# A fused attention and feed-forward kernel: bias rows stored in two goes, sums issued before copies, the first x split by VectorE

## The chip, the cores and the metric

The kernel runs on one core of a Trainium2 chip. Its engines are TensorE (PE in the profile; PEld is its weight load), VectorE (DVE), ScalarE (ACT), GpSimd (POOL) and SyncE (SP), which here only issues transfers. The metric is the device time of one execution in microseconds; a lower time is better.

## What is computed

Attention with a learned bias of position, 4 batches (B), 8 heads (H), 576 positions (S), head size 64 (D), and behind it a gated feed-forward layer over the 2304 resulting rows of 512 features:

```python
scores = scale * np.matmul(q, k.transpose(0, 1, 3, 2))
x = (psi_rel / psi_i)[..., None]
h = np.maximum(x @ w1 + b1, 0.0)
bias = h @ w2                                  # S x S x heads
scores = scores + bias.transpose(2, 0, 1)[None, :, :, :]
attn = np.exp(scores - np.max(scores, axis=-1, keepdims=True))
attn = attn / (np.sum(attn, axis=-1, keepdims=True) + 1e-09)
out = np.matmul(attn, v)                       # (B, H, S, D), then (B*S, H*D) as x
h = x @ w_in
sp = np.log1p(np.exp(h))
y = (h * np.tanh(sp)) @ w_out
```

All arrays are float32. Where full accuracy is wanted, a factor is split into a high and a low part, and a product is three matmuls (high x high, high x low, low x high).

## The kernel before, in words

The program is written out in order, engine by engine: each engine runs its instructions in the order in which the Python code records them, and waits on semaphores. Nothing reorders them. Transfers are issued in order by SP; each waits for one that was issued eight before it to land, and for the data it reads.

**Bias table** (to about 57 us). 36 tiles of 16 positions are made by `make_h` (ACT and DVE), a matmul, and `evac` (L471), which scales the result into a tile `bt` of 128 rows (16 positions x 8 heads) x 591 floats and stores it to `bias_d[c]`, one DRAM tensor for each of the chunks of 128 query positions (the last has 64). The chunks go in `ORDER` 0, 1, 4, 2, 3. `load_bias(hp, c)` reads the two heads of a head pair back; for head pair 0 (heads 0 and 1) the calls stand at the numbers in `BIAS_AT`. The first three steps of the attention already run in here.

**Attention** (to about 320 us). 16 pairs i (head pair, batch), 5 chunks each, so steps n = 0 to 79 (`NS` = 80). Of a step, `scores` (PE) makes the products, `add_bias` (DVE, L209; "the sums" below) adds the bias and takes the row's least value, `exps` (ACT, L224) the exponentials and their totals, `transposes` two steps later turns them on PE and copies them to SBUF (ACT L265, L267, L270, L271; in step 3 one of the copies on DVE), `pv_duo` (PE) multiplies with v, and its result is copied by DVE (L291) and stored to `x_d`. PSUM holds one step's scores and one result at a time. `reciprocals` (DVE L231 to L234) turns a pair's totals into factors, which go to `r_d`. In between, `split` takes a weight through a conversion of DVE steps (L118, L121, L123, L125). Step 3 is written apart: PE's three earlier transposes and the first products are recorded ahead of its sums.

**x for the feed-forward part.** x is worked on in five blocks of 512 tokens (block 2 has 256). `load_x` reads a block, `load_r` its factors, broadcast over 64 partitions; x times the factors is split into `x_hi` and `x_lo`. For block 0 this happens during the last eleven steps of the attention (`ahead`, L327), in halves: POOL multiplies (L346), DVE casts to the high part (L349), POOL subtracts (L350). For the others it happens in the block before (`split_x`, L536; DVE and ACT), load at f = 6 and parts from f = 8 on, f being the number of the unit's first 128 features of 2048.

**Feed-forward part** (from about 310 us). Units of one f (in block 2 two) run through `hidden` (L554), `gate` (L572) and, three units later, `project` (L588). At the end of a block the four results are copied by DVE and ACT in turn and stored; the very last tile is copied in halves by both engines (L611, L612).

Of the kernel before, what the change touches and what calls it, by code (L numbers as in the profile page):

```python
# [19 lines left out]
P = 128  # L20
# [24 lines left out]
def kernel(ctx: ExitStack, tc, qk, v, wb, w2, w_in, w_out, psia, psi4, rinv, eye, out):  # L45
# [101 lines left out]
    st = lsbuf("st", 6)  # L147
    rawp = rsbuf("raw", 2, side="right")
    biasp = rsbuf("biasp", side="right")
    s_ps = rpsum("s_ps", 2, side="right")  # L150
    qk_raw, v_t, bias_t = {}, {}, {}
    st.tile([P, 32], F32, name="fill", bufs=1)
# [146 lines left out]
    conv = []  # L299
    alloc_weights(order[:EARLY], wpool)  # L300

    x_raw, x_r, x_hi, x_lo = {}, {}, {}, {}
    blocks = [(0, 512), (512, 512), (1024, 256), (1280, 512), (1792, 512)]

    def load_x(blk, p):
# [21 lines left out]
    def ahead(n):  # L327

        i, x = divmod(n, 5)
        if x == 0 and i + 1 < NPAIR:  # L330
            load_raw(i + 1)
        if i % B == B - 1 and i // B + 1 < HP:
            load_bias(i // B + 1, ORDER[x])
        if n == NS - 11:
            load_x(0, x0)
        if n in (NS - 10, NS - 8):
            x_r[0] = x0.tile([P, 2, TB], F32, name="xr", bufs=1)
            h0 = 0 if n == NS - 10 else 2
            load_r(0, x_r[0], h0, h0 + 2)
        if n in (NS - 9, NS - 7):  # L340
            if n == NS - 9:
                x_hi[0] = xa.tile([P, HP, TB], F32R, name="xhi")
                x_lo[0] = xa.tile([P, HP, TB], F32R, name="xlo")
            h0 = 0 if n == NS - 9 else 2
            for d in range(2):
                pool.tensor_tensor(x_raw[0][:, h0 + d], x_raw[0][:, h0 + d], x_r[0][:, d], op=ALU.mult)  # L346
        if n in (NS - 7, NS - 6, NS - 4, NS - 3):
            d = (NS - 7, NS - 6, NS - 4, NS - 3).index(n)
            dve.tensor_copy(x_hi[0][:, d], x_raw[0][:, d])  # L349
            pool.tensor_tensor(x_lo[0][:, d], x_raw[0][:, d], x_hi[0][:, d].bitcast(F32), op=ALU.subtract)  # L350

    def split(n):

# [10 lines left out]
    def step(n):  # L364
        i, x = divmod(n, 5)

        def begin():
            if n < NS:
                scores(n)
                add_bias(n)  # L370
                exps(n, 0)

        def turn():
            if 0 <= n - LAG < NS:
                transposes(n - LAG)

        def end():
            if n < NS:
                ahead(n)
                split(n)  # L380
            if 0 <= n - 1 < NS and (n - 1) % 5 == 4:
                reciprocals((n - 1) // 5)

        def products():
            todo = {4: (i, 0, (0, 1)), 0: (i - 1, 0, (2, 3)), 1: (i - 1, 0, (4,)), 2: (i - 1, 1, (0, 1, 2)),
                    3: (i - 1, 1, (3, 4))}.get(x, (-1, 0, ()))
            j, grp, ks = todo
            if 0 <= j < NPAIR and (j, grp) != (0, 0):
                for k in ks:
                    pv_duo(j, grp, k)  # L390

        if n in (3, 4):
            scores(n)
            if n == 3:
                for k in range(3):
                    transposes(k, True)
                for k in range(5):
                    pv_duo(0, 0, k)
            add_bias(n)
            exps(n, 0)  # L400
            exps(n, 1)
            end()
            return
        begin()
        turn()
        if n < NS:
            exps(n, 1)
        end()
        products()

# [18 lines left out]
    dve.tensor_scalar(bb, psi4_t, wbt[:, 1:2], None, op0=ALU.mult)  # L429
    dve.tensor_scalar(at, at, wbt[:, 0:1], None, op0=ALU.mult)  # L430
    ts = [t for c in ORDER for t in range(8 * c, min(8 * c + 8, S // 16))]
    bps_t, h_t = {}, {}
    NB = len(ts)
    NW = S + 15

# [7 lines left out]
    spent = {"v": 0.0, "a": 0.0}  # L443
    maker = {}
    SOFT_AT = (18, 27, 32)
    BIAS_AT = (12, 20, 24, 36, 37)
    for idx, t in enumerate(ts):
        spent["a"] += 1.0 + (1.9 if idx in SOFT_AT else 0.0)
        spent["v"] += (1.7 if idx in SOFT_AT else 0.0)
# [21 lines left out]
    def evac(idx):  # L471
        t = ts[idx]
        ps = bps_t.pop(t)
        bt = bo.tile([P, NW], F32, name="bt")
        left, right, _ = reach(t)
        if idx > NB - 3:
            dve.tensor_scalar(bt[:, :left], ps[:, left:0:-1], rinv_t[:, t:t + 1], None, op0=ALU.mult)
        else:
            act.mul(bt[:, :left], ps[:, left:0:-1], rinv_t[:, t:t + 1])
        act.mul(bt[:, left:], ps[:, :right], rinv_t[:, t:t + 1])  # L480

        c = t // 8
        a = (16 * t - P * c) * PITCH + PAD - 15
        dst = bias_d[c][:, a:a + 16 * (PITCH + 1)].rearrange("h (i j) -> i h j", j=PITCH + 1)
        sp.dma_start(out=dst[:, :, :NW], in_=bt)

    make_h(0)
    make_h(1)
# [1 line left out]
    for idx in range(NB + 2):  # L490
        if idx < NB:
            t = ts[idx]
            make_h(idx + 2)
            n = reach(t)[2]
            ps = bps.tile([P, 1024], F32, name="bps")
            for a in range(0, n, 512):
                for cg in range(4):
                    pe.matmul(ps[cg * 32:cg * 32 + 32, a:min(a + 512, n)], w2t,
                              h_t[idx, cg][:, a:min(a + 512, n)], start=True, stop=True)
            bps_t[t] = ps  # L500
        if 1 <= idx <= NB:
            evac(idx - 1)
        if idx == 1:
            load_raw(0)
        if idx in BIAS_AT:
            load_bias(0, ORDER[BIAS_AT.index(idx)])
        for lag, do in enumerate((scores, add_bias, exps)):
            if idx - lag in SOFT_AT:
                for u in range(2 if lag == 2 else 1):
                    do(SOFT_AT.index(idx - lag), *((u,) if lag == 2 else ()))  # L510
        if idx == 14:
            load_raw(1)
        if idx == 26:
            load_weights()
    bias_scope.close()

    ptp = lsbuf("ptp", 1)
# [70 lines left out]
    def project(blk, fs):  # L588
# [13 lines left out]
        if fs[-1] == NFC - 1:  # L602
            for t in range(nt):
# [5 lines left out]
                if blk == len(blocks) - 1 and t == nt - 1:  # L609

                    dve.tensor_copy(part[:, :DM // 2], ys[blk][t][:, :DM // 2])  # L611
                    act.copy(part[:, DM // 2:], ys[blk][t][:, DM // 2:])  # L612
                    sp.dma_start(out=rows[:, :DM // 2], in_=part[:, :DM // 2])
                    act.dma_start(out=rows[:, DM // 2:], in_=part[:, DM // 2:])
                    continue
                if t % 2:
                    act.copy(part, ys[blk][t])
# [23 lines left out]
    for k in range(2, len(units) + LAG2):  # L641
        if k < len(units):
            blk, fs = units[k]
            f = fs[0]
            if blk + 1 < len(blocks):
                if f == 6:
                    load_x(blk + 1, xp)
                    x_lo[blk + 1] = (xa if blk % 2 else xp).tile([P, HP, TB], F32R, name="xlo")
                    load_r(blk + 1, x_lo[blk + 1].bitcast(F32), 0, HP)

                if f >= 8:
                    split_x(blk + 1, XPARTS[f - 8:f - 8 + len(fs)])
            if k > 2:
                hidden(blk, fs)
        if k >= LAG2:
            project(*units[k - LAG2])
        if 2 <= k - 1 < len(units):
            gate(*units[k - 1], 2)
# [55 lines left out]
```

## Time and profile before

| | us |
|---|---|
| three runs, median | 723.97 |
| the three runs | 723.97, 726.0, 722.36 |
| the profiled execution, its own time | 719.21 |
| its span, first to last instruction | 717.4 |
| busy: PE | 689.8 |
| busy: DVE, ACT, POOL | 513.1, 480.6, 19.5 |

The span is what the views divide up; 1.8 us of the execution lie around it. Matmuls are pipelined and their ends modelled, so PE's busy time counts a matmul that crawls at a lowered clock as busy too; the granted clock (PEclk, 1.00 is full speed) stands beside it. "Idle before" in a row is the time in which that engine stood still just before the instruction, with what ended it.

### The profile page before, as it was taken

How to read it: one execution, taken by the hardware profiler on the slowest of the kernel's cores; microseconds unless marked ns; L12 is line 12 of the kernel's file. 1: busy time of each engine (PE TensorE's matmuls, PEld its weight loads, DVE VectorE, ACT ScalarE, POOL GpSimd, SP SyncE). 2: the span in 40 equal slices, each digit the busy share in tenths (PEclk: the TensorE clock that was granted, in tenths of full speed). 3: DMA queues.
4: the chain of work that ended last, by engine and by line, in shares of the span. 5: the costliest groups of instructions: out<-in, count | busy, mean ns of one | idle time of the engine just before them, and what ended most of it. 6: DMA issues, size and time to landing. Idle time of an engine off the chain costs nothing.

```text
span 717.4 us, 12816 instructions
## 1 busy us (share of the span) xinstructions
PE 689.8 (96%) x4768; PEld 506.6 (71%) x4768; DVE 513.1 (72%) x1082; ACT 480.6 (67%) x1051; POOL 19.5 (3%) x20
## 2 busy tenths in 40 slices
PE   6778999999999999899999999999999999999997
PEld 2225666666666666568888888889978888888886
DVE  7996887788888787758779665665476567565564
ACT  6886998898899989776666454544454554454443
POOL 0000100000000000501000000000000000000000
PEclk9999999999999999999999999999999999999999
DMA  5996458447646846104000030000604100010001
GB/s 157 323 322 198 178 193 259 157 140 248 206 158 219 262 166 221 47 18 127 1 0 1 1 117 1 0 1 6 172 1 124 24 0 1 1 58 1 1 1 58
DMA packets 43919, 74.79 MB, mean 104 GB/s; under 512 B 13905, under 2 KB 22609, under 8 KB 43857
## 3 DMA queue, kind: packets, MB, share of 16 engines
q1 hardware_dynamic: 43280, 73.75, 31.8%
q8 instruction: 37, 0.61, 0.3%
q10 hardware_dynamic: 576, 0.22, 0.1%
q14 instruction: 26, 0.20, 0.1%
HBM read 53.55 MB, written 20.40 MB: 103 GB/s over the span
## 4 chain that ended last, share of the span: by engine, by line
PE 68%; ACT 12%; DVE 6%; DMA 4%; issue 3%; SPq 1%; POOL 0%; DVEq 0%; ACTq 0%
PE y L600 25%; PE h L562 25%; PE s L193 6%; PE o L284 6%; ACT pt L224 5%; ACT main L265 3%; PE tp L257 3%; DVE pt L209 2%; PE tp L260 1%; PE o L288 1%; DMA r_d<-rt 1%; DMA xlo<-r_d 1%; DMA xraw<-x_d 1%; DMA bias_d<-bt 1%; ACT main L270 1%
## 5 line engine op out<-in xcount | busy, mean ns | idle before, releaser
L209 DVE CUSTOM_DVE_ANT_0 pt<-s,bias 128x576 f32<-128x576 f32 (+1 forms) x160 | 115.8, 754 | 45.2 <-PE s L193 44.0
L224 ACT ACTIVATE pt<-pt,m 128x576 f32<-128x576 f32 x144 | 111.2, 773 | 24.5 <-DVE m L209 19.8
L600 PE MATMUL y<-who,glo 128*128 128x512 f32 x288 | 112.2, 389 | 0.0
L600 PE MATMUL y<-who,ghi 128*128 128x512 f32 x288 | 112.2, 389 | 0.0
L600 PE MATMUL y<-wlo,ghi 128*128 128x512 f32 x288 | 112.1, 389 | 0.0
L193 PE MATMUL s<-rawqk 64*128 64x288 f32 x640 | 109.6, 432 | 2.0 <-DVE m L209 2.0
L584 ACT CAST ghi<-e 128x512 fp32r<-128x512 f32 x72 | 44.7, 621 | 92.6 <-DVE e L580 92.6
L193 PEld LDWEIGHTS s<-rawqk 64*128 64x128 f32 x640 | 64.0, 186 | 44.5 <-DVE m L209 16.5
L567 ACT ACTIVATE e<-h 128x512 f32<-128x512 f32 x72 | 42.9, 596 | 64.0 <-PE h L562 63.7
L585 DVE TENSOR_TENSOR glo<-e,ghi 128x512 fp32r<-128x512 f32 x72 | 49.8, 691 | 44.9 <-ACT ghi L584 44.9
L568 DVE TENSOR_SCALAR e<-e 128x512 f32<-128x512 f32 x72 | 30.6, 425 | 71.6 <-ACT e L567 71.6
L562 PE MATMUL h<-xlo,whi 128*128 128x512 f32 (+1 forms) x320 | 79.3, 368 | 1.0 <-DVE xlo L546 0.9
L562 PE MATMUL h<-xhi,whi 128*128 128x512 f32 (+1 forms) x320 | 79.0, 369 | 0.0
L284 PE MATMUL o<-main,vt 128*64 128x320 f32 (+1 forms) x512 | 75.9, 418 | 3.1 <-DVE x L291 3.1
L562 PE MATMUL h<-xhi,wli 128*128 128x512 f32 (+1 forms) x320 | 78.7, 368 | 0.0
L257 PEld LDWEIGHTS tp<-ident,pt 64*128 64x128 f32 x1184 | 55.9, 139 | 18.0 <-ACT main L265 8.3
L265 ACT COPY main<-tp 128x512 f32<-128x512 f32 x126 | 66.7, 578 | 2.0 <-DMA bias_d<-bt 1.0
L562 PEld LDWEIGHTS h<-xhi,whi 128*128 128x128 f32 x320 | 57.1, 188 | 11.7 <-issue 0.5
L562 PEld LDWEIGHTS h<-xlo,whi 128*128 128x128 f32 x320 | 56.9, 189 | 11.6 <-DVE xlo L546 1.7
L257 PE MATMUL tp<-ident,pt 64*128 64x64 f32 x1184 | 62.0, 227 | 2.6 <-ACT main L265 1.2
L562 PEld LDWEIGHTS h<-xhi,wli 128*128 128x128 f32 x320 | 56.9, 189 | 10.0
L600 PEld LDWEIGHTS y<-who,glo 128*128 128x128 f32 x288 | 54.1, 188 | 11.8 <-DVE glo L585 0.4
(58 smaller groups left out, 890.6 us busy)
## 6 DMA issues: line engine op xcount, KB each, us to landing
rawqk<-in_qk_dram SPq DMA_DIRECT2D x16, 672.0 KB
bias_d<-bt SPq DMA_DIRECT2D x36, 295.5 KB
w<-in_w_in_dram SPq DMA_DIRECT2D x16, 512.0 KB
w<-in_w_out_dram SPq DMA_DIRECT2D x16, 512.0 KB
vt<-in_v_dram SPq DMA_DIRECT2D x16, 320.0 KB
bias<-bias_d SPq DMA_DIRECT2D x16, 288.0 KB
out_dram<-w SPq DMA_DIRECT2D x17, 256.0 KB
bias<-bias_d SPq DMA_DIRECT2D x16, 256.0 KB
```

The source lines that it names most:

```text
L193: pe.matmul(s[:, j, :SH], q[rows], raw[rows, k0 + j * SH:k0 + (j + 1) * SH], start=True, stop=True)
L209: dve.tensor_tensor_reduce(out=halves(pt[rows, sl]), in0=s[rows, :, :SH], in1=halves(bt[rows, sl]), scale=-0.125, scalar=BIG, op0=ALU.add, ...
L224: act.activation(ps, ps, AF.Exp, bias=m[:, u:u + 1], scale=-1.0, accum_out=sums[i][:, k:k + 1])
L257: pe.transpose(tp[:, k * 64:k * 64 + 64], pt[rows, c0:c0 + P], ident[rows, rows])
L265: copy(main[:, :, :, q0:q0 + 64], tp.rearrange("p (h k q) -> p h k q", h=2, k=4))
L284: pe.matmul(o[h * 64:h * 64 + 64, :w], vt[:, h, k, :], main[:, h, k, :], start=(k == 0), stop=False, **kw)
L562: pe.matmul(h[:, u * n:(u + 1) * n], w["i", g4, d][:, r * P:(r + 1) * P], x[:, d, :n], start=(k == 0), stop=(k == 11))
L567: act.activation(e, h, AF.Exp)
L568: dve.tensor_scalar(e, e, E20, None, op0=ALU.min)
L584: act.copy(ghi, e)
L585: dve.tensor_tensor(glo, e, ghi.bitcast(F32), op=ALU.subtract)
L600: pe.matmul(ys[blk][t], g[:, c0:c0 + P], w, start=(f == 0 and k == 0), stop=(f == NFC - 1 and k == 2))
```

## The change

1. **Bias stores.** The last six tiles (numbers 30 to 35, all of chunk 3) lie in a pool of their own, `latep`, which outlives the table. Heads 0 and 1 of each are stored first, by two transfers of 16 rows. All eight heads are stored once more after the loop, behind the load of chunk 3.
2. **`BIAS_AT`.** The load of chunk 2 stands two tiles earlier (34 for 36).
3. **Steps 3 and 4.** The sums of step 3 stand behind the first of three transposes; exponentials and transposes alternate; the first pair's products move to step 4, behind its sums.
4. **`end()`.** Reciprocals are recorded ahead of the step's loads and weight steps.
5. **First x.** One load of all factors, into `x_lo`; at steps 75 to 78 DVE multiplies x by them straight into `x_hi`, POOL multiplies x in place and subtracts.
6. **Last pair.** Its third product of group 0 moves one step up.
7. **Last copy.** ACT's half goes to a tile of its own.
8. **Block 3.** In block 2 the next block's load stands at f = 2 and its parts from f = 6.

```diff
-    BIAS_AT = (12, 20, 24, 36, 37)
+    BIAS_AT = (12, 20, 24, 34, 37)
...
+        late = idx >= NB - 6
+        bt = (latep if late else bo).tile([P, NW], F32, name="late" if late else "bt")
...
-        sp.dma_start(out=dst[:, :, :NW], in_=bt)
+        if late:
+            rows = bt.rearrange("(i h) j -> i h j", h=H)
+            for h in range(2):
+                sp.dma_start(out=dst[:, h, :NW], in_=rows[:, h])
+            again.append((dst[:, :, :NW], bt))
+        else:
+            sp.dma_start(out=dst[:, :, :NW], in_=bt)
...
+    for rows, bt in again:
+        sp.dma_start(out=rows, in_=bt)
     bias_scope.close()
...
             if n == 3:
-                for k in range(3):
-                    transposes(k, True)
+                transposes(0, True)
+            add_bias(n)
+            exps(n, 0)
+            if n == 3:
+                transposes(1, True)
+            exps(n, 1)
+            if n == 3:
+                transposes(2)
+            else:
                 for k in range(5):
                     pv_duo(0, 0, k)
-            add_bias(n)
-            exps(n, 0)
-            exps(n, 1)
             end()
...
+            if 0 <= n - 1 < NS and (n - 1) % 5 == 4:
+                reciprocals((n - 1) // 5)
             if n < NS:
                 ahead(n)
                 split(n)
-            if 0 <= n - 1 < NS and (n - 1) % 5 == 4:
-                reciprocals((n - 1) // 5)
...
-        if n in (NS - 10, NS - 8):
-            x_r[0] = x0.tile([P, 2, TB], F32, name="xr", bufs=1)
-            h0 = 0 if n == NS - 10 else 2
-            load_r(0, x_r[0], h0, h0 + 2)
-        if n in (NS - 9, NS - 7):
...
-            for d in range(2):
-                pool.tensor_tensor(x_raw[0][:, h0 + d], x_raw[0][:, h0 + d], x_r[0][:, d], op=ALU.mult)
-        if n in (NS - 7, NS - 6, NS - 4, NS - 3):
-            d = (NS - 7, NS - 6, NS - 4, NS - 3).index(n)
-            dve.tensor_copy(x_hi[0][:, d], x_raw[0][:, d])
-            pool.tensor_tensor(x_lo[0][:, d], x_raw[0][:, d], x_hi[0][:, d].bitcast(F32), op=ALU.subtract)
+        if n == NS - 10:
+            x_hi[0] = xa.tile([P, HP, TB], F32R, name="xhi")
+            x_lo[0] = xa.tile([P, HP, TB], F32R, name="xlo")
+            load_r(0, x_lo[0].bitcast(F32), 0, HP)
+        if NS - 5 <= n < NS - 1:
+            d = n - (NS - 5)
+            x, hi, lo = (y[0][:, d] for y in (x_raw, x_hi, x_lo))
+            dve.tensor_tensor(hi, x, lo.bitcast(F32), op=ALU.mult)
+            pool.tensor_tensor(x, x, lo.bitcast(F32), op=ALU.mult)
+            pool.tensor_tensor(lo, x, hi.bitcast(F32), op=ALU.subtract)
...
-                if f == 6:
+                early = 2 * (len(fs) - 1)
+                if f == 6 - 2 * early:
                     load_x(blk + 1, xp)
...
-                if f >= 8:
-                    split_x(blk + 1, XPARTS[f - 8:f - 8 + len(fs)])
+                if f >= 8 - early:
+                    split_x(blk + 1, XPARTS[f - 8 + early:f - 8 + early + len(fs)])
```

How the order moves at three places (rows of the built programs; the first column is the line in that version's code, which lies one line lower from the attention on and up to ten lower at the end after the change).

SP at the end of the table, before: `bias_d_81` is chunk 3's tensor, `bias_852` and `bias_856` the loaded chunks 2 and 3.

```order
L485 DMA bias_d_81<-bt 16x8x591 x8
L168 DMA bias_852<-bias_d_80 128x576
L169 DMA bias_852<-bias_d_80 128x512
L170 DMA bias_852<-bias_d_80 128x64
L168 DMA bias_856<-bias_d_81 128x576
L169 DMA bias_856<-bias_d_81 128x512
L170 DMA bias_856<-bias_d_81 128x64
L293 DMA x_d_83<-x 128x256
```

And after, where the two chunks are `bias_845` and `bias_865`:

```order
L492 DMA bias_d_81<-bt 16x8x591 x2
L489 DMA bias_d_81<-late 16x591 x8
L169 DMA bias_845<-bias_d_80 128x576
L170 DMA bias_845<-bias_d_80 128x512
L171 DMA bias_845<-bias_d_80 128x64
L489 DMA bias_d_81<-late 16x591 x4
L169 DMA bias_865<-bias_d_81 128x576
L170 DMA bias_865<-bias_d_81 128x512
L171 DMA bias_865<-bias_d_81 128x64
L523 DMA bias_d_81<-late 16x8x591 x6
L294 DMA x_d_83<-x 128x256
```

Chunk 2's load now has four small stores behind it that stood, as two whole ones, ahead of it; six whole stores come behind chunk 3's load.

DVE at steps 3 and 4, before (a sum is two rows, its second reads the row's least value):

```order
L265 COPY main_888<-tp 128x8x64 x2
L291 COPY x<-o 128x256
L209 ISA pt,m<-s,bias_852 128x576
L209 ISA m 128x1
L209 ISA pt,m<-s,bias_852 128x576
L209 ISA m 128x1
L118 TENSOR_SCALAR w_978<-w_684 128x512
L121 TENSOR_SCALAR w_684<-w_684 128x512
L209 ISA pt,m<-s,bias_856 128x576
```

And after:

```order
L266 COPY main_903<-tp 128x8x64
L210 ISA pt,m<-s,bias_845 128x576
L210 ISA m 128x1
L210 ISA pt,m<-s,bias_845 128x576
L210 ISA m 128x1
L266 COPY main_903<-tp 128x8x64
L118 TENSOR_SCALAR w_979<-w_687 128x512
L121 TENSOR_SCALAR w_687<-w_687 128x512
L210 ISA pt,m<-s,bias_865 128x576
```

Step 3's sums stand ahead of the second copy and of the copy of the products' result, which comes only after step 4's sums.

DVE at steps 73 to 75, before:

```order
L349 CAST xhi<-xraw 128x512
L123 SCALAR_TENSOR_TENSOR w_4280<-w_4280,w_4124 128x512
L125 SCALAR_TENSOR_TENSOR w_4280<-w_4124,w_4280 128x512
L291 COPY x<-o 128x320
L209 ISA pt,m<-s,bias_3645 128x576
L209 ISA m 128x1
L209 ISA pt,m<-s,bias_3645 128x576
L209 ISA m 128x1
L349 CAST xhi<-xraw 128x512
```

And after, at step 73:

```order
L210 ISA pt,m<-s,bias_3613 128x576
L210 ISA m 128x1
L123 SCALAR_TENSOR_TENSOR w_4289<-w_4289,w_4139 128x512
L125 SCALAR_TENSOR_TENSOR w_4289<-w_4139,w_4289 128x512
L292 COPY x<-o 128x320
```

and after, at step 75:

```order
L210 ISA pt,m<-s,bias_3466 128x576
L210 ISA m 128x1
L232 TENSOR_SCALAR sums<-sums 128x9
L233 RECIPROCAL rpad_884<-sums 128x9
L235 STREAM_TRANSPOSE rt<-rpad_884 128x32
L344 TENSOR_TENSOR xhi<-xraw,xlo 128x512
```

No cast stands ahead of the weight steps any more; the first multiplication closes step 75, behind the reciprocals.

ACT at the very end, after, with the semaphores that a row waits for:

```order
L593 CAST ghi<-e 128x512 [waits DVE_49,PE_49]
L627 COPY w_7804<-y_7279 128x512 [waits DMAHW7_49,DMAHW6_49,PE_49]
L622 COPY r<-y_7281 128x256 [waits DVE_49]
L624 DMA out_dram<-r 128x256 [waits DMAHW5_49,Activation_49]
L721 UNCONDITIONAL_BRANCH
```

The last copy (L612 before, L622 here) waited for transfers and for DVE, and now for DVE alone.

## Rows read from the trace of the kernel before

**Rows 1.** Page, part 1: busy us, share of the span, instructions of each engine
```profile
PE 689.8 (96%) x4768; PEld 506.6 (71%) x4768; DVE 513.1 (72%) x1082; ACT 480.6 (67%) x1051; POOL 19.5 (3%) x20
```

**Rows 2.** Busy time by window, the first line naming the columns
```profile
core 0: us, PE busy (x) PEld busy (x) DVE busy (x) ACT busy (x) POOL busy (x), PEclk, DMA share, GB/s
52.00:72.00 20.00, 16.86 (x158) 9.26 (x152) 13.36 (x34) 12.48 (x33) 1.46 (x3) 1.00 0.68 216
...
269.20:285.10 15.90, 15.75 (x164) 10.27 (x162) 12.59 (x33) 14.91 (x41) 0.00 (x0) 1.00 0.68 231
285.10:301.10 16.00, 13.74 (x129) 9.33 (x129) 11.11 (x26) 11.64 (x32) 7.47 (x6) 0.89 0.25 63
```

**Rows 3.** Chain that ended last, end of the bias table: start us, us, what
```profile
51.94 5.37 DMA bias_d<-bt
```

**Rows 4.** Timeline, same place: start, us, engine, line, operation, [idle before <- releaser]
```profile
53.99 0.52 SPq L485 DMA_DIRECT2D bias_d<-bt  x1
...
55.01 1.24 PE L193 MATMUL s<-rawqk 64*128 64x288 f32 x8
...
56.97 0.58 SPq L168 DMA_DIRECT2D bias<-bias_d  x1
...
58.96 0.58 ACT L265 COPY main<-tp 128x512 f32<-128x512 f32 x1 [0.55 <-PE tp L257]
...
59.44 0.53 ACT L267 COPY tail<-tp 64x128 f32<-64x128 f32 x2
...
59.60 0.69 PE L257 MATMUL tp<-ident,pt 64*128 64x64 f32 x10 [0.28 <-ACT main L265]
...
60.19 0.32 SPq L168 DMA_DIRECT2D bias<-bias_d  x1
...
60.22 1.95 PE L284 MATMUL o<-main,vt 128*64 128x256 f32 x16
...
62.65 0.42 DVE L291 COPY x<-o 128x256 f32<-128x256 f32 x1 [2.93 <-PE o L288]
...
63.78 0.78 ACT L224 ACTIVATE pt<-pt,m 128x576 f32<-128x576 f32 x1 [2.31 <-DVE m L209]
...
66.64 0.69 DVE L123 SCALAR_TENSOR_TENSOR w<-w,w 128x512 uint32<-128x512 uint32 x1
...
67.97 0.75 DVE L209 CUSTOM_DVE_ANT_0 pt<-s,bias 128x576 f32<-128x576 f32 x1
```

**Rows 5.** Timeline, last quarter of the attention, where the first x is scaled
```profile
287.62 2.50 POOL L346 TENSOR_TENSOR xraw<-xraw,xr 128x512 f32<-128x512 f32 x2 [194.03 <-DMA r_d<-rt]
...
288.93 1.47 DVE L349 CAST xhi<-xraw 128x512 fp32r<-128x512 f32 x1 [1.07 <-POOL xraw L346]
...
290.15 1.24 SPq L323 DMA_DIRECT2D xr<-r_d  x2
...
292.19 1.08 PE L284 MATMUL o<-main,vt 128*64 128x256 f32 x8 [2.26 <-DVE x L291]
...
295.06 2.51 POOL L346 TENSOR_TENSOR xraw<-xraw,xr 128x512 f32<-128x512 f32 x2 [4.94 <-DMA xr<-r_d]
...
295.65 0.75 DVE L209 CUSTOM_DVE_ANT_0 pt<-s,bias 128x576 f32<-128x576 f32 x1
...
296.33 1.26 DVE L231 TENSOR_SCALAR sums<-sums 128x9 f32<-128x9 f32 x1
```

**Rows 6.** Timeline, PE at the second group of the last pair's products
```profile
320.92 2.38 PE L284 MATMUL o<-main,vt 128*64 128x320 f32 x16 [0.85 <-DVE x L291]
```

**Rows 7.** Timeline, block 2 of the feed-forward part, split of block 3
```profile
502.98 1.26 SPq L309 DMA_DIRECT2D xraw<-x_d  x2
...
514.34 1.29 DVE L543 TENSOR_TENSOR xraw<-xraw,xlo 128x512 f32<-128x512 f32 x2 [4.54 <-DMA xlo<-r_d]
...
532.93 1.10 PE L562 MATMUL h<-xlo,whi 128*128 128x512 f32 x2 [0.89 <-DVE xlo L546]
```

**Rows 8.** Timeline, ScalarE's last copy
```profile
714.07 0.37 ACT L612 COPY w<-y 128x256 f32<-128x256 f32 x1 [1.23 <-DVE w L611]
```

More of the change, by code (lines that the diff above doesn't have):

```diff
@@ L149 @@
     biasp = rsbuf("biasp", side="right")
+    latep = rsbuf("late", 6, side="right")
     s_ps = rpsum("s_ps", 2, side="right")
@@ L300 @@
     alloc_weights(order[:EARLY], wpool)
-    x_raw, x_r, x_hi, x_lo = {}, {}, {}, {}
+    x_raw, x_hi, x_lo = {}, {}, {}
     blocks = [(0, 512), (512, 512), (1024, 256), (1280, 512), (1792, 512)]
@@ L335, in ahead @@
             load_x(0, x0)
-        if n in (NS - 10, NS - 8):
-            x_r[0] = x0.tile([P, 2, TB], F32, name="xr", bufs=1)
-            h0 = 0 if n == NS - 10 else 2
-            load_r(0, x_r[0], h0, h0 + 2)
-        if n in (NS - 9, NS - 7):
[L341 to L344, printed above, removed]
-            for d in range(2):
-                pool.tensor_tensor(x_raw[0][:, h0 + d], x_raw[0][:, h0 + d], x_r[0][:, d], op=ALU.mult)
-        if n in (NS - 7, NS - 6, NS - 4, NS - 3):
-            d = (NS - 7, NS - 6, NS - 4, NS - 3).index(n)
-            dve.tensor_copy(x_hi[0][:, d], x_raw[0][:, d])
-            pool.tensor_tensor(x_lo[0][:, d], x_raw[0][:, d], x_hi[0][:, d].bitcast(F32), op=ALU.subtract)
+        if n == NS - 10:
[8 more added lines that the diff above has]
+            pool.tensor_tensor(lo, x, hi.bitcast(F32), op=ALU.subtract)
     def split(n):
@@ L380, in end @@
                 split(n)
-            if 0 <= n - 1 < NS and (n - 1) % 5 == 4:
-                reciprocals((n - 1) // 5)
         def products():
-            todo = {4: (i, 0, (0, 1)), 0: (i - 1, 0, (2, 3)), 1: (i - 1, 0, (4,)), 2: (i - 1, 1, (0, 1, 2)),
+            todo = {4: (i, 0, (0, 1)), 0: (i - 1, 0, (2, 3) if i < NPAIR else (2, 3, 4)), 1: (i - 1, 0, (4,) if i < NPAIR else ()), 2: (i - 1, 1, (0, 1, 2)),
                     3: (i - 1, 1, (3, 4))}.get(x, (-1, 0, ()))
@@ L431 @@
     ts = [t for c in ORDER for t in range(8 * c, min(8 * c + 8, S // 16))]
-    bps_t, h_t = {}, {}
+    bps_t, h_t, again = {}, {}, []
     NB = len(ts)
@@ L473, in evac @@
         ps = bps_t.pop(t)
-        bt = bo.tile([P, NW], F32, name="bt")
+        late = idx >= NB - 6
+        bt = (latep if late else bo).tile([P, NW], F32, name="late" if late else "bt")
         left, right, _ = reach(t)
@@ L611, in project @@
                     dve.tensor_copy(part[:, :DM // 2], ys[blk][t][:, :DM // 2])
-                    act.copy(part[:, DM // 2:], ys[blk][t][:, DM // 2:])
+                    rest = mp.tile([P, TB], F32, name="r")[:, :DM // 2]
+                    act.copy(rest, ys[blk][t][:, DM // 2:])
                     sp.dma_start(out=rows[:, :DM // 2], in_=part[:, :DM // 2])
-                    act.dma_start(out=rows[:, DM // 2:], in_=part[:, DM // 2:])
+                    act.dma_start(out=rows[:, DM // 2:], in_=rest)
                     continue
```

## The prediction

> **What bounds the kernel now.** I read the page's part 1 first: TensorE (PE) is busy for 689.8 of 717.4 us [rows 1], so whatever takes less work off another engine is worth nothing unless PE stood still for it, and 27.6 us is all the standing there is. Next I asked for busy time by window, to see where PE stands and the change reaches. Between 52 and 72 us PE lacks 3.14 us [rows 2]. A regular pair of heads fills its 15.90 us but for 0.15, while the pair from 285.1 on lacks 2.26 us, and its granted clock is 0.89 instead of 1.00 [rows 2]. Two more holes are single waits: 0.85 us at 320 us [rows 6] and 0.89 us at 533 us [rows 7]. The rest is the bias table, the start and the end. These four holes are what the edits touch, so I read each of them in the timeline, and asked which wait ends last.
>
> **End of the bias table (stores apart, sums ahead of copies, one load earlier).** The table's rows go out through the DMA queues, which carry a backlog: a store begun at 51.94 landed 5.37 us later [rows 3], and the first copies of the attention waited for it, because their tiles lie where the store's source lay. Then VectorE (DVE) makes its two copies and waits 2.93 us for PE's products before it copies their result at 62.65; only behind that, in its own order, stand the sums of step 3, and ScalarE (ACT) had waited 2.31 us for them when it began their exponentials at 63.78 [rows 4].
> After: six tiles lie elsewhere, so the first copies start when their transposes end, taken as 57.2, a little before the 57.31 at which that store released them. Of the six, a quarter of the bytes (heads 0 and 1) is stored first. A whole tile is 128 rows of 591 floats, 303 KB, so 6 x 227 KB, 1.36 MB, leaves the queue ahead of the two loads. The load of chunk 2 moves ahead of the last two tiles' stores: tile 33 was stored at 53.99, the load issued at 56.97 [rows 4]; now it follows tile 33 at about 54.8. The sums of step 3 can then run behind one copy (0.58 on ACT, taken as 0.7 on DVE), at 57.9. From there, by rows 4: two sums 1.4 (the first done at 58.6), exponential 0.78 (59.4), copies of the second transposes 0.58 + 0.53 (60.5), third transposes 0.69 (61.2), scores of step 4 as at 55.01, 1.24 (62.4), products as from 60.22 to 62.65, 2.43 (64.9), the copy 0.4, then L123 and L125, which took from 66.64 to 67.97, 1.33 (66.6). The sums of step 5 come next; they began at 67.97. **Gain 1.3 us.** DVE works almost without a gap from 62.65 on before, so the shift reaches PE.
> The unknown is when chunk 2 lands. Before it was there by the time its sums ran, at 63.0, 6.0 us after issue; that is the late end, and gives 60.8 now. The early end is no wait at all (57.9, 3.1 us after issue). I take the early end, as the nearest row is the last store: it was issued just ahead of 56.97 and the load that waits for it went at 60.19 [rows 4], some 3.2 us and more, in a fuller queue. Late would turn +1.3 into -1.6. Below that the gain ends at the 3.14 us that PE lacks there.
> Added: twelve small stores ahead, at up to 0.52 us of SP's time each [rows 4], in place of six large ones; six whole tiles again (1.82 MB) behind chunk 3's load. SP now waits for that load before it issues them, and behind them stand the result's store, one weight load, the reciprocals' stores and the next q and k. At 216 GB/s [rows 2] the 1.82 MB take 8.4 us, and q and k are first read a whole pair, some 16 us, later: hidden. If that cover went, each us late would be a us of PE.
>
> **First x.** Before, GpSimd (POOL) multiplied, DVE made the high part from the product, POOL the rest. POOL could only start when the factors had landed, 287.62; DVE's cast at 288.93 stood 1.07 us idle for it and then took 1.47 us; behind it in DVE's order lay two weight steps, the copy of a result, and the next sums, so PE waited 2.26 us for that copy [rows 5]. The clock then fell to the lower of its two levels (1.2 of 2.4 GHz) for a while: a mean of 0.89 over 16.0 us loses 1.76 us of PE's work. Together 2.26 + 1.76 - 0.15 of a regular pair = 3.87. After: nothing of x stands in DVE's order before step 75 (of 80), and then DVE multiplies by itself (four operations in place of four casts), at the end of a step, where sums already issued let PE go on. It waits only for the load. The load is now one, of both halves: the first half had landed by 287.6, the second alone took from 290.15 to 295.06, 4.9 us, at most [rows 5], so it is there by 292.5. The first multiplication comes where the reciprocal line L231 stood, 296.33 [rows 5], less 3.8, plus about 0.6 for the reciprocals that now go first: 293.1. **Gain 3.8 us.**
> What is added: POOL now does two operations a step, four steps running, 2.5 us of each 3.2 us step (a fifth of the regular pair; two of POOL's operations took 2.50 and 2.51 [rows 2, 5]). Does that block DVE? The row that speaks: a sum at 295.65 took its usual 0.75 us in the middle of POOL's pair from 295.06 to 297.57, but L231 at 296.33, a small operation from SBUF to SBUF, took 1.26 us and ended with POOL's [rows 5]. So sums run beside POOL and some others don't. DVE's multiplication comes a whole step after the last one released POOL, 3.2 us against 2.5, so they should miss each other.
> The Trainium skill, page "SBUF — State Buffer", section "Who interferes with whom", says that a VectorE instruction with two SBUF inputs contends with a GpSimd instruction that reads SBUF, and that the one that comes second waits for the first to finish. By that rule the new multiplication is open to such a hold; the cast's 1.47 us beside POOL agrees that holds exist, and rival 2 has the price.
>
> **Last pair's products, one matmul pair earlier.** PE stood 0.85 us for a copy [rows 6], since one PSUM buffer holds both groups. The copy now comes a unit earlier, but the products also need ACT's copies of the last transposes, which in the trace end just before; PE's work only changes places. I take 0.1, between 0 and 0.85.
>
> **Block 3 of x.** Its load was issued at 502.98, its first user waited 4.54 us for it until 514.34, and at 532.93 PE waited 0.89 us for the last low part [rows 7]. Between load and that wait lie five units of block 2, so a unit is 6 us at most. The load moves two units ahead and the split one, so the user gets one unit more, above the 4.54 it lacked, and the split ends a unit before block 3. **Gain 0.9 us**; SP is idle at the load's new place and only results' stores stand behind it.
>
> **No effect:** ScalarE's last copy writes a tile of its own, but in the built program it still waits for a VectorE instruction, and the PSUM tile is still read by both, so the 1.23 us of idle [rows 8] stay. The reciprocals stand earlier in DVE's order by the length of two weight steps; their four small stores now precede the next q and k on SP, which have a pair's time in hand. Zero; DVE is 72% busy [rows 1], and that covers it.
>
> **Sum.** 3.8 + 1.3 + 0.9 + 0.1 = 6.1 us. The profiled execution took 719.21 us (717.4 of span and 1.8 around it), and would take 713.1. It is 4.8 below the median of the three runs shown, 723.97; taken off that, **717.9 us**.
>
> **Rivals.** (1) *The bias still comes late.* Two copies and both later transposes now stand behind sums that wait for chunk 2. If it lands at 60.8, this part costs 1.6 instead of giving 1.3: 720.8. For it: the queue's backlog of 5.37 us [rows 3]; against: 1.36 MB less ahead of it. (2) *POOL holds DVE.* Four multiplications each held for one POOL operation, 1.25 us, are 5 us of DVE, of which I let half reach PE, as DVE has about 30% of the pair free [rows 2]: 717.9 + 2.5 = 720.4. For: L231's 1.26; against: the step is longer than POOL's pair. The rule of the Trainium skill above gives this time if every one collides. (3) *Slower: the x load misses its place.* DVE stands in front of the sums of step 76 until all of it has landed; each us past 293.1 is a us of PE, and after a wait the clock falls again (1.76). From 293.1 + 6.1 - 1.8 = 297.4 on the kernel is slower than before; landing at 301 gives 727.5. Against: the 292.5 above. (4) *The last copy does run beside the other*: 0.4 us more, 717.5; the wait in the program speaks against it.
>
> **How the numbers follow.** Forecast 0.70 (with 4 in it), rival 1 0.10, rival 2 0.13, rival 3 0.05, more gain than I see 0.02. Low end: all 3.14 us of the first hole and all 0.85 of the third, 715.3, and somewhat less for the spread of the runs (722.36 to 726.0): 714.5. High end: rivals 1 and 2 with half of that spread, 721.8. A measurement of this kernel tells about 0.5%, 3.6 us, from no change; faster than 720.35 are nearly all of the forecast and under half of rivals 1 and 2: 0.75; slower 0.05, the rest 0.20.
>
> **What would show it.** Right: the sums of step 3 before PE's first products, the load of chunk 2 near 55; no PE wait over 0.5 us between 285 and 300 and a clock of 1.00 there; no wait of PE on xlo in block 3's first unit; the tail as before. Wrong: a VectorE wait on bias before step 3's sums, multiplications of 1.5 us or more, or VectorE waiting for xlo's load at step 75.

## The result: the total as forecast, from other terms

| | before | after |
|---|---|---|
| median | 722.36 us | 717.57 us |
| runs | 721.91 to 726.0 | 716.01 to 718.15 |
| profiled execution, its span | 719.21, 717.4 | 716.97, 715.2 |

The ratio is 0.9917, 95% interval 0.989 to 0.9945: faster by 0.8%, at the 717.9 us that was forecast. Yet the profiled executions lie only 2.2 us apart, where the sum had 6.1. So the terms have to be read one by one.

**End of the bias table.** Busy time and clock by 2 us, after (window, length, busy PE, PEld, DVE, ACT and POOL with counts, granted clock, DMA share, GB/s):

```profile
56.00:58.00 2.00, 1.61 (x23) 0.96 (x19) 0.78 (x2) 1.07 (x3) 0.00 (x0) 1.00 0.23 73
58.00:60.00 2.00, 1.12 (x18) 0.74 (x18) 0.01 (x1) 0.26 (x1) 0.00 (x0) 1.00 0.36 61
60.00:62.00 2.00, 0.00 (x0) 0.00 (x0) 0.62 (x1) 0.00 (x0) 0.00 (x0) 0.94 0.85 304
62.00:64.00 2.00, 0.37 (x2) 0.19 (x3) 1.83 (x7) 1.78 (x6) 0.00 (x0) 0.50 0.21 45
64.00:66.00 2.00, 2.00 (x15) 1.89 (x17) 0.35 (x2) 1.88 (x6) 0.00 (x0) 0.50 0.87 278
66.00:68.00 2.00, 2.00 (x10) 0.77 (x8) 1.25 (x3) 0.45 (x1) 0.00 (x0) 0.50 0.13 25
68.00:70.00 2.00, 2.00 (x18) 1.05 (x14) 0.19 (x2) 1.18 (x4) 0.00 (x0) 0.85 0.92 271
```

PE does nothing at all from 60 to 62, and then its clock stands at the lower level for 6 us. The DMA share is 0.23 and 0.36 just before: no backlog by then. ScalarE's first copy of the attention, SP's issues and VectorE's first sum of step 3, in the timeline of after (start, length, engine, line, operation, tiles):

```profile
50.48 7.71 SPq L489 DMA_DIRECT2D bias_d<-late  x8
...
57.26 0.58 ACT L266 COPY main<-tp 128x512 f32<-128x512 f32 x1 [0.79 <-PE tp L258]
...
58.23 0.58 SPq L169 DMA_DIRECT2D bias<-bias_d  x1
...
62.98 0.33 SPq L169 DMA_DIRECT2D bias<-bias_d  x1
...
61.38 0.76 DVE L210 CUSTOM_DVE_ANT_0 pt<-s,bias 128x576 f32<-128x576 f32 x1 [3.36 <-DMA bias<-bias_d]
```

SP's waits in after, 40 to 75 us (engine, line, what it waited for: us in total, times, longest):

```profile
SPq L489 <- DMA bias_d<-bt: 1.9, 4, 0.9
SPq L489 <- DMA w<-in_w_in_dram: 1.6, 2, 0.8
```

Every transfer on SP waits for the one issued eight before it to land. The eight small stores ahead of chunk 2's load therefore wait, one for one, for eight older transfers: two loads of weights and whole stores. SP lost 3.5 us in these waits in this execution. The load of chunk 2 behind them went out at 58.23, not at 54.8, and its data came 3.15 us later. Copies and transposes now stood behind sums that waited for it. What this cost is read from a mark that both programs have, VectorE's first sum of the next 64-row step, in the timeline of before:

```profile
73.50 0.75 DVE L209 CUSTOM_DVE_ANT_0 pt<-s,bias 64x576 f32<-64x576 f32 x1 [0.26 <-PE s L193]
```

and in that of after:

```profile
77.27 0.75 DVE L210 CUSTOM_DVE_ANT_0 pt<-s,bias 64x576 f32<-64x576 f32 x1 [0.26 <-PE s L194]
```

3.77 us later; at the step before the hole (51.97, now 52.16) it was 0.19. So this execution lost 3.6 us against that of before, where 1.3 were to be gained.

**First x.** The window of after that answers [rows 2]:

```profile
285.10:301.10 16.00, 15.86 (x166) 10.38 (x165) 11.54 (x31) 15.00 (x40) 2.55 (x2) 1.00 0.56 156
```

VectorE's multiplications, and one of GpSimd's operations, in its timeline:

```profile
297.72 0.65 DVE L344 TENSOR_TENSOR xhi<-xraw,xlo 128x512 fp32r<-128x512 f32 x1
...
299.80 1.28 POOL L346 TENSOR_TENSOR xlo<-xraw,xhi 128x512 fp32r<-128x512 f32 x1
...
300.43 1.20 DVE L344 TENSOR_TENSOR xhi<-xraw,xlo 128x512 fp32r<-128x512 f32 x1
...
303.46 1.42 DVE L344 TENSOR_TENSOR xhi<-xraw,xlo 128x512 fp32r<-128x512 f32 x1
...
307.31 0.82 DVE L344 TENSOR_TENSOR xhi<-xraw,xlo 128x512 fp32r<-128x512 f32 x1
```

PE lacks 0.14 of the 16 us where it lacked 2.26, at a clock of 1.00 for 0.89. The first multiplication (297.72) has no wait in front of it: the load was there. Between 286 and 309 us the sums went from 3.63 us late to 0.14 early: 3.77 us gained.

**The rest.** Timeline of after, PE at the last pair, PE in the first unit of block 3, and ScalarE's last copy; they answer [rows 6], [rows 7] and [rows 8]:

```profile
320.60 2.37 PE L285 MATMUL o<-main,vt 128*64 128x320 f32 x16 [0.82 <-ACT main L266]
...
529.02 1.07 PE L571 MATMUL h<-xhi,whi 128*128 128x512 f32 x4
529.92 1.07 PE L571 MATMUL h<-xhi,wli 128*128 128x512 f32 x4
530.83 1.07 PE L571 MATMUL h<-xlo,whi 128*128 128x512 f32 x4
531.74 0.39 PE L609 MATMUL y<-who,ghi 128*128 128x512 f32 x1
...
711.92 0.37 ACT L622 COPY r<-y 128x256 f32<-128x256 f32 x1 [1.23 <-DVE w L620]
```

The wait at 320 us has changed its releaser (ScalarE's copy for VectorE's), not its length. Block 3 no longer waits. The last copy waits 1.23 us as it did.

### The profile page after: what moved, and what is told of

It is laid out like the page before. It is cut to its first block, busy times and chain, and to the rows that moved or that the text cites. A ratio compares the mean times of both kernels' runs of the same rounds, so it can differ in the third digit from the quotient of the medians.

```text
span 715.2 us, 12810 instructions
## 1 busy us (share of the span) xinstructions
PE 687.8 (96%) x4768; PEld 505.8 (71%) x4768; DVE 513.6 (72%) x1082; ACT 480.4 (67%) x1051; POOL 22.6 (3%) x20
## 4 chain that ended last, share of the span: by engine, by line
PE 77%; ACT 13%; DVE 4%; DMA 3%; issue 2%; SPq 0%; ACTq 0%; DVEq 0%
PE h L571 28%; PE y L609 27%; PE s L194 7%; PE o L285 6%; ACT pt L225 6%; ACT main L266 3%; PE tp L258 3%; PE bps L505 3%; DVE pt L210 2%; PE tp L261 2%; PE o L289 1%; DMA bias_d<-bt 1%; DMA w<-in_w_in_dram 1%; DVE ht L468 1%; ACT main L271 1%
## 5 line engine op out<-in xcount | busy, mean ns | idle before, releaser
L194 PE MATMUL s<-rawqk 64*128 64x288 f32 x640 | 108.0, 432 | 0.7 <-DVE m L210 0.7
```

Of the source, the lines that this page charges most:

```text
L194: pe.matmul(s[:, j, :SH], q[rows], raw[rows, k0 + j * SH:k0 + (j + 1) * SH], start=True, stop=True)
```

## Experiments

Every run is compared with runs of the kernel before on the same chip, whose medians were 721.93, 721.91, 721.96 and 722.61 us in the four sessions. Marks are starts of VectorE's sums against the profiled execution of before (+ is later): the one at 83.68 us stands behind the bias table, those at 286.42 and 309.43 on either side of the first x. Between the first two marks some executions lose another 1.5 us, e2, e5 and e6 among them; what is lost near 180 us is read below the table. A median is uncertain by the scatter of four to twelve runs: a difference between two of these kernels by some 1 to 1.5 us.

| kernel | median us (runs) | ratio, 95% interval | 83.68 | 286.42 | 309.43 | span |
|---|---|---|---|---|---|---|
| after | 717.57 (5) | 0.9917, 0.989 to 0.9945 | +3.77 | +3.63 | -0.14 | 715.2 |
| e1 table's end as before | 717.15 (6) | 0.9928, 0.9902 to 0.9955 | +4.27 | +3.80 | +0.07 | 715.3 |
| e2 stores apart, old order | 715.02 (6) | 0.9898, 0.9873 to 0.9922 | -0.27 | +1.20 | -2.55 | 712.8 |
| e3 whole stores, sums ahead | 717.84 (6) | 0.9935, 0.9912 to 0.9958 | +4.44 | +4.59 | +0.84 | 716.1 |
| e4 first x only | 718.50 (12) | 0.9946, 0.9924 to 0.9967 | +1.89 | +1.94 | -1.80 | 715.4 |
| e5 sums between | 716.13 (7) | 0.9914, 0.988 to 0.9947 | +1.99 | +3.48 | -0.28 | 715.0 |
| e6 after, weights early | 714.95 (6) | 0.9898, 0.9866 to 0.993 | +1.73 | +3.20 | -0.55 | 714.7 |
| e7 e5, weights early | 714.37 (6) | 0.9885, 0.9852 to 0.9919 | +1.05 | +1.72 | -2.04 | 713.3 |
| e8 e2, block 3 as before | 716.73 (8) | 0.9929, 0.9903 to 0.9956 | +0.63 | +0.72 | -3.03 | 714.1 |
| e9 e2, weights early | 715.25 (4) | 0.9905, 0.9885 to 0.9924 | +3.00 | +3.84 | +0.07 | 715.4 |
| e10 e1, weights early | 713.14 (4) | 0.9882, 0.9863 to 0.9902 | -0.04 | -0.03 | -3.80 | 711.5 |
| e11 before, weights early | 719.49 (7) | 0.9956, 0.9941 to 0.9971 | +1.33 | +0.66 | +0.86 | 718.7 |

**Between the first two marks: the reciprocals.** The forecast gave their new place no effect. In the timeline of before SP issues the load of a weight ahead of a pair's factors, and VectorE's first step of its conversion has no wait:

```profile
167.67 0.38 SPq L104 DMA_DIRECT2D w<-in_w_in_dram  x1
168.15 2.72 SPq L236 DMA_DIRECT2D r_d<-rt  x4
...
176.82 0.42 DVE L118 TENSOR_SCALAR w<-w 128x512 f32<-128x512 f32 x1
```

In that of e5 the factors' stores go first, after 3.6 us in which SP waited for their data, and the weight's load, with those of q, k, v and bias ahead of it, some 4 us later by the marks. VectorE then waits for that weight, and TensorE for a copy that VectorE makes behind it:

```profile
168.35 1.35 SPq L237 DMA_DIRECT2D r_d<-rt  x4
...
173.62 0.53 SPq L104 DMA_DIRECT2D w<-in_w_in_dram  x1
...
180.65 0.43 DVE L118 TENSOR_SCALAR w<-w 128x512 f32<-128x512 f32 x1 [2.12 <-DMA w<-in_w_in_dram]
...
181.54 1.08 PE L285 MATMUL o<-main,vt 128*64 128x256 f32 x8 [1.53 <-DVE x L292]
```

VectorE's wait stands in all ten kernels that have the reciprocals' new place (0.51 to 2.12 us) and in none of the three that haven't (before, e4, e11). By the sums from 174.85 to 186.60 us of before it cost 0 to 1.6 us of the time: nothing in after, 0.5 in e2 and e10, 1.3 in e6, 1.6 in e5. No run changes the reciprocals alone.

**e1: what the new end of the table is worth.** Stores and `BIAS_AT` put back as here, and the order of steps 3 and 4 as under e2; the rest of the change kept.

```diff
-    BIAS_AT = (12, 20, 24, 34, 37)
+    BIAS_AT = (12, 20, 24, 36, 37)
...
-        if late:
-            rows = bt.rearrange("(i h) j -> i h j", h=H)
-            for h in range(2):
-                sp.dma_start(out=dst[:, h, :NW], in_=rows[:, h])
-            again.append((dst[:, :, :NW], bt))
-        else:
-            sp.dma_start(out=dst[:, :, :NW], in_=bt)
+        sp.dma_start(out=dst[:, :, :NW], in_=bt)
...
-    for rows, bt in again:
-        sp.dma_start(out=rows, in_=bt)
```

> The changed kernel with the end of the bias table put back: whole stores, the load of chunk 2 at its old place, sums of steps 3 and 4 behind all copies and products; everything else of the change stays. Theory from the two traces: sums of the 64-row step after the table ran 0.2 us later than before at 52 us and 3.8 us later at 77 us, so the new end of the table costs 3.6 us and the rest gives 5.8. Then this kernel takes 717.6 - 3.6 = 714.0 us, and its trace has no stretch near 61 us in which TensorE does nothing and no lower clock there. Rival (the forecast's own term): the new end gives 1.3 us in most executions, and the profiled one of before was a lucky one, as it lies 3.2 us under its median: 718.9 us.

717.15 us: neither theory's number, and my first theory fell. The old end, instruction for instruction that of before, was 4.27 us late here and 1.89 late in e4 (below). VectorE's first copy of the attention, in the timeline of e1:

```profile
59.41 0.69 DVE L265 COPY main<-tp 128x512 f32<-128x512 f32 x1 [3.50 <-DMA bias_d<-bt]
```

in that of e4:

```profile
57.95 0.69 DVE L265 COPY main<-tp 128x512 f32<-128x512 f32 x1 [1.70 <-DMA bias_d<-bt]
```

and the store that e1's chain of waits names for it (start, length, what):

```profile
51.96 7.23 DMA bias_d<-bt
```

In before that store took 5.37 us [rows 3], and the copy began at 57.53. In e1 PE stood still for it from 58 to 60, and the clock fell (windows of e1):

```profile
58.00:60.00 2.00, 0.07 (x1) 0.08 (x1) 0.59 (x1) 0.71 (x2) 0.00 (x0) 0.86 1.01 307
60.00:62.00 2.00, 1.98 (x19) 1.37 (x19) 0.79 (x2) 1.01 (x4) 0.18 (x2) 0.50 0.60 215
```

So the profiled execution of before, on which the sum was built, was a lucky one at this very place, as far as these two others can tell.

**e2 and e3: stores or order.** e2 puts back only the order, as here, e3 only stores and `BIAS_AT`, as in the diff of e1:

```diff
             if n == 3:
-                transposes(0, True)
+                for k in range(3):
+                    transposes(k, True)
+                for k in range(5):
+                    pv_duo(0, 0, k)
             add_bias(n)
             exps(n, 0)
-            if n == 3:
-                transposes(1, True)
             exps(n, 1)
-            if n == 3:
-                transposes(2)
-            else:
-                for k in range(5):
-                    pv_duo(0, 0, k)
```

> The changed kernel with the order of sums, copies and products in steps 3 and 4 put back, but the small stores, the stores again and the earlier place of chunk 2's load kept. If the loss comes from the order alone (TensorE has no products to do while the sums wait for chunk 2), this takes about 714 us, or 713 if the free tiles let the first copies start earlier. If it comes from the small stores (the load of chunk 2 issued at 58.2 instead of 57.0, chunk 3's at 63.0 instead of 60.2), the sums of step 3 run at 62.6 as before but those of step 4 come some 2.8 us later: about 716.5 to 717.6 us.

> The changed kernel with whole stores and the old place of chunk 2's load, but with the sums of steps 3 and 4 ahead of copies and products. If the order is the cause, the sums of step 3 wait for chunk 2 until about 60.2 (issued at 56.97, 3.1 us to land), TensorE stands idle meanwhile and its clock falls again: 716.5 to 717.6 us. If the small stores are the cause, this takes 714.0 us or less.

715.02 and 717.84 us. The stores apart are good: 2.1 us less than e1. The order is bad: with the stores apart it costs 2.55 (717.57 less 715.02); the 0.7 that it costs without them is within the noise. Together they are worth -0.4, and nothing that can be told from zero. The window from 60 to 62 us in e2, where PE has products to do while the sums wait:

```profile
60.00:62.00 2.00, 2.00 (x21) 1.28 (x20) 0.00 (x0) 1.15 (x4) 0.00 (x0) 1.00 0.33 66
```

The small stores aren't always as late as in the execution of after. In e2, with the same stores in the same place, SP shows no wait for a landing between 44 and 60 us, and chunk 2's load went out 2.4 us earlier (timeline of e2):

```profile
55.80 0.58 SPq L169 DMA_DIRECT2D bias<-bias_d  x1
```

In e5 below it went out at 56.66, behind 1.6 us of such waits.

**e4: first x alone**, put into the kernel before:

```diff
-            dve.tensor_copy(x_hi[0][:, d], x_raw[0][:, d])
...
+            load_r(0, x_lo[0].bitcast(F32), 0, HP)
+        if NS - 5 <= n < NS - 1:
...
+            dve.tensor_tensor(hi, x, lo.bitcast(F32), op=ALU.mult)
```

> The kernel before with only the first x changed (one load of all factors, VectorE's multiplication into the high part, GpSimd's product and difference at steps 75 to 78). By the marks in the two traces (sums 3.63 us later at 287 us, 0.14 earlier at 306 to 310) this part gives 3.8 us: 722.4 - 3.8 = 718.6 us. Rival: part of the loss there was one execution's, and typical executions gain only the idle time of 2.26 us: 720.1 us.

718.50, 3.4 us less. By the marks it gives 3.74, and in each of the ten other kernels that have it 3.73 to 3.77: the step of the forecast that held best.

**e5 to e7: what the sums wait for.** e5, against e2:

```diff
             if n == 3:
                 for k in range(3):
                     transposes(k, True)
+            add_bias(n)
+            if n == 3:
                 for k in range(5):
                     pv_duo(0, 0, k)
-            add_bias(n)
             exps(n, 0)
```

e6 and e7 move the weights' first loads, in after and in e5:

```diff
-        if idx == 26:
+        if idx == 0:
             load_weights()
```

> The changed kernel, stores apart kept, but the sums of step 3 placed between its copies and its products instead of ahead of both (steps 4 as before the change). In the run with the stores apart and the old order VectorE was idle for 2.9 us before the result's copy, while the products ran. Theory: the loss of the changed order comes only from copies and transposes that stand behind sums which wait for chunk 2, so that TensorE runs dry and its clock falls; here TensorE has the products meanwhile, and the sums come up to 1.3 us earlier than in the old order: 715.0 - 1.3 = 713.7 us. Rival: sums earlier are worth nothing, since the scores of step 4 stand behind the products all the same: 715.0 us.

> The changed kernel with the first weights' two loads (0.5 MB each) issued at the start, when the queues are nearly idle (share 0.01 from 4 to 8 us), instead of in the middle of the last stores. Their landing is what the third and fourth small store wait for (1.6 us in all), and the load of chunk 2 stands behind these on SyncE. Theory (chunk 2 comes too late for the new order): it is issued 2 us or more earlier, the sums of step 3 wait less than 1 us, TensorE has no empty 2 us near 61, and the time falls to 714 to 715 us. Rival (the order itself is bad, whenever chunk 2 comes): 717 to 718 us.

> The two runs beside this one together: stores apart, sums of step 3 between copies and products, the first weights loaded at the start. If both earlier sums and a shorter queue give something, this is the fastest: 713.0 us, and the sums of step 3 don't wait for chunk 2 at all. If the queue no longer matters once the sums stand behind the copies, it equals the run with the sums between: 713.7 us.

e5 missed, 716.13 instead of 713.7, which is not to be told from e2's 715.02: the sums of step 3 did come at 59.59, but those of step 4 then waited for chunk 3, in the timeline of e5:

```profile
64.59 0.76 DVE L210 CUSTOM_DVE_ANT_0 pt<-s,bias 128x576 f32<-128x576 f32 x1 [1.14 <-DMA bias<-bias_d]
...
66.81 0.76 DVE L210 CUSTOM_DVE_ANT_0 pt<-s,bias 128x576 f32<-128x576 f32 x1 [1.45 <-DMA bias<-bias_d]
```

The sums of step 3 in the timeline of e6:

```profile
59.87 0.76 DVE L210 CUSTOM_DVE_ANT_0 pt<-s,bias 128x576 f32<-128x576 f32 x1 [0.19 <-DMA bias<-bias_d]
...
61.02 0.76 DVE L210 CUSTOM_DVE_ANT_0 pt<-s,bias 128x576 f32<-128x576 f32 x1 [0.39 <-DMA bias<-bias_d]
```

e6 took 714.95, as expected for a late chunk 2: with its load at 56.97 the wait of 3.36 us shrinks to 0.19 and 0.39, and the 2.55 us that the order cost are back. With the weights early the order costs nothing: e9 (below), which differs from e6 by the old order alone, took 715.25. e7, at 714.37, is near its 713.7; that it differs from e6 or e2 isn't shown.

**e8: block 3.** Load and split at their old places, on top of e2:

```diff
-                early = 2 * (len(fs) - 1)
-                if f == 6 - 2 * early:
+                if f == 6:
...
-                if f >= 8 - early:
+                if f >= 8:
```

> The run with the stores apart and the old order of steps 3 and 4 (715.0 us), with the load and split of block 3's x put back to their old places. The forecast had 0.9 us for it, the idle time of TensorE in one row: 715.9 us. The traces show the first hidden unit of block 3 taking 4.25 us before and 2.72 after, 1.5 us: two of the matrix products after the wait took twice their time. By that 716.5 us.

716.73: 1.7 us, nearer to the 1.5 read from the unit than to the 0.9 of the idle time. The medians alone can't tell these two apart, but the table can: from the mark at 309.43 to the end of the span lie 405.8 to 405.9 us in the nine kernels with the early split and 407.7 to 408.4 in the four without (before, e4, e8, e11); between e2 and e8 it is 1.8. In the timeline of e8 the wait is back:

```profile
529.73 1.10 PE L567 MATMUL h<-xlo,whi 128*128 128x512 f32 x2 [0.86 <-DVE xlo L551]
```

Two products take 1.10 us there; four in a row take 1.07. Why they do is open; the granted clock was 1.00 in both windows that hold them (528 to 532 us).

**e9 to e11: is it the backlog?** The weights' loads at the start, in e2, in e1, and in the kernel before.

> Stores apart, the old order of steps 3 and 4, and the first weights' two loads at the start. The run with the sums between showed the wait move on to chunk 3 (1.1 and 1.5 us before the sums of step 4), so earlier sums are worth nothing while chunk 3 lands at 65 to 67; the old order asks for chunk 3 last. Theory: this is as fast as the fastest so far or faster, 713.5 to 714.4 us, and neither VectorE nor TensorE waits for a bias load between 55 and 70 us. Rival (sums early do give something once the queue is short): 715.0 us, as with the stores apart alone.

> The run with the end of the bias table as before (717.2 us), with the first weights' two loads at the start. In three executions of these same stores the one begun near 51.95 landed after 5.4 us or over 7, and the first copies, which write where its source lies, began between 57.5 and 60 us; where TensorE stood for it, its clock fell. Theory (the lateness is the queue's backlog, of which the weights are 1 MB): the copies start by 57.5, the clock stays, 714.0 to 715.0 us. Rival (it is not the backlog, but what a store of this shape takes): the copies start as late as before and the time stays at 717.2.

> The kernel before, with nothing changed but the first weights' two loads, issued at the start instead of at tile 26. Theory: what made the old end of the table late in typical executions (its copies began between 57.5 and 60 us, and the clock fell where TensorE stood for them) is the backlog that these 1 MB add; the run with all other parts of the change gained 4.0 us by the same edit, so 722.0 - 4.0 = 718.0 us, with a narrower spread than 718.5 to 727.4. Rival: the gain needs the other edits (the first x lies 220 us later, so it should not): 721 to 722 us.

e10 has the lowest median, 713.14 us, below the 714.0 to 715.0 expected: every one of its runs (712.34 to 714.72) lies under the fastest of the changed kernel (that it beats e7 isn't shown). Its first copies wait for PE only, no longer for a store (timeline of e10):

```profile
57.48 0.69 DVE L265 COPY main<-tp 128x512 f32<-128x512 f32 x1 [1.22 <-PE tp L257]
```

The queues are less full there: from 52 to 58 us the DMA share is 0.82, 0.67 and 0.80 in e10, where e1 has 1.04, 1.04 and 0.99. In the kernel before the same line gives 3.1 us of the 4.0 expected, with runs from 719.19 to 720.43. e9 missed (715.25, as e2): in its profiled execution, the slowest of its four, the clock had fallen at 50 to 54 us already, inside the table, before any bias load matters, and it fell again at 66 to 72. The first sum inside the table was 1.86 us late by the first fall; 1.5 more came with the second. e6 shows the first fall, and so does e8, whose weights come late (0.65 and 0.50 from 48 to 52 us); e7 doesn't. So early weights aren't its condition; what is, is open. Nor is it settled whether e9 is slower than e10 for its stores or for these falls.

## Why the forecast came out right

- **The start, 723.97 us.** The forecast took the profiled execution's 4.8 us under the median of three runs for a constant and added it to its result. Longer series put before at 721.9 to 722.6: the start was 1.4 to 2.1 us too high. (The high end of the range, 721.8, doesn't follow from its terms either: rival 1's 720.8 and half of the runs' 3.6 us make 722.6. Nothing hangs on it here.)
- **First x, 3.8.** Right: 3.4 by medians, 3.77 by marks, clock and idle time as told. "They should miss each other" was wrong: three of four multiplications were held beside GpSimd (0.82 to 1.42 us instead of 0.65, 1.5 us in all), but under the 1.5 us each that would have shown rival 2, and nearly all of it in VectorE's slack: the sums slipped by 0.2 us (from 0.28 early at 299.34 of before to 0.05 at 301.93). This agrees with the Trainium skill, page "SBUF — State Buffer", section "Who interferes with whom", by which the instruction that comes second waits for the first: the one at 300.43 ends 0.55 us after GpSimd's, which began first and ended at 301.08.
- **End of the table, 1.3.** Wrong. Two of its terms held: the first copies began at 57.26 (57.2 forecast), and chunk 2 was there 3.15 us after its issue (3.1). The step that failed is "now it follows tile 33 at about 54.8": the bytes in the queue were counted, not that the eight small stores ahead of the load take eight of SP's turns, each behind a landing eight transfers back. It was issued at 58.23; in e2, where no landing was waited for, at 55.80, still 1.0 us later than forecast. Rival 1 (data at 60.8) had the late sums, though from a slow landing, and priced them at 1.6; in the trace it is 3.6, as the empty 2 us also lower the clock. The sign that was named for it, VectorE waiting on bias before step 3's sums, is there with 3.36 us. By medians the part is worth -0.4, because the old end is itself late in the other executions that were traced (e1, e4), which the single trace of before didn't show.
- **Block 3, 0.9.** Right in its mechanism, too small: 1.7 by medians, 1.8 by the marks. The idle time in the row leaves out two products that ran at half their pace behind it.
- **Last pair, 0.1, and no effect from the last copy.** As told, by the rows above (0.82 for 0.85, 1.23 for 1.23); no run of its own was made for them. From the last mark to the end, e8, which has them, and e4, which hasn't, agree within 0.1 us.
- **Reciprocals, zero.** Held in the profiled execution of after, not in others: 0 to 1.6 us lost near 180 us. The forecast saw their stores ahead of the next q and k, which can wait, but not ahead of a weight's load, which VectorE wants some 5 us after it now goes out.

In sum, 3.4 + 1.7 - 0.4 + 0.1 = 4.8 us, the measured difference, in place of 6.1. (The first three are medians with more than 1 us of noise each, and the reciprocals are left out, so that they meet it to a tenth is chance.) The error of 1.3 in the sum was hidden by the error in the start. That the number came out is luck: two of the four terms, a zero and the start were off, and the errors all but cancelled.

## What to carry to other kernels

A transfer cut in two is two turns in an ordered queue with a fixed number in flight: count turns and the landings that they wait for, not only bytes. A store moved ahead of loads in such a queue holds them all up until its data are ready. Before sums are put ahead of an engine's other work, ask when their data land, and leave that engine something to do until then; better still, move what clogs the queue (here 1 MB of weights that nobody needed yet) into a time when it is idle. And a profiled execution below the median may be lucky at the very place that one wants to improve: the gap is no constant to be added to a forecast.

## What was not expected of the hardware

The same work with the same idle time doesn't always keep the clock. From 62 to 64 us PE was busy for 0.80 of 2 us in before, in e10 and in e11; of these three in e11 alone the clock then fell, to 0.86 and 0.50 (windows of before, then of e11):

```profile
62.00:64.00 2.00, 0.80 (x7) 0.34 (x4) 1.35 (x4) 0.22 (x1) 0.00 (x0) 1.00 0.66 240
64.00:66.00 2.00, 1.71 (x8) 0.77 (x7) 1.82 (x7) 1.40 (x4) 0.00 (x0) 1.00 0.19 64
66.00:68.00 2.00, 1.90 (x17) 1.27 (x19) 1.97 (x7) 1.63 (x4) 0.00 (x0) 1.00 0.01 4
...
62.00:64.00 2.00, 0.80 (x7) 0.31 (x4) 1.48 (x4) 0.35 (x1) 0.00 (x0) 1.00 0.79 282
64.00:66.00 2.00, 1.62 (x9) 0.70 (x7) 1.82 (x7) 1.33 (x5) 0.00 (x0) 0.86 0.14 42
66.00:68.00 2.00, 2.00 (x7) 1.82 (x9) 1.90 (x4) 1.62 (x5) 0.00 (x0) 0.50 0.02 4
```

The same hole kept the clock in e2 and in e4 (there from 64 to 66 us) and lost it in e9 (from 64 to 66, then 0.86 and 0.50). In e11 the fall cost some 1.4 us: its sums were 0.12 us ahead of before at 63.66 and 1.33 behind at 71.88. So a part of what two single executions differ by is not the edit's.

And the store begun near 51.95 us, the same instruction in the same place, landed after 5.37 us in one execution and after 7.23 in another.
